# A written order for attention's instructions, value products in one block, and a rounded query that a transfer copies

## The chip, the cores and the metric

The kernel runs on one core of a Trainium2 chip. The metric is the device time of one execution in microseconds, the median of several runs; before the change it is 939.33 us (three runs, 938.42 to 941.68).

## What is computed

Three blocks follow each other on a batch of 4 sequences of 576 tokens. Attention with a decay has 8 heads of 64 per sequence, so 32 heads in all:

```
scores = scale * q @ k^T ; decay = cum[i] - cum[j], cum = cumsum(log(clip(f)))
attn   = exp(masked(scores + decay) - max) ; attn /= sum + 1e-9 ; out = attn @ v
```

Then comes a Fourier mixing over tokens and channels with a normalisation and a two-layer feed-forward (`u + relu(un @ w_ch1) @ w_ch2`), and last a block that multiplies by cos and sin of `x @ w_theta`, mixes over tokens with two 576 x 576 matrices, and gates. Every matmul in which 32-bit accuracy counts is split into high and low rounded parts.

## The kernel before, in words

`phase1` does attention and the Fourier transforms, `phase2` the feed-forward, `phase3` the last block. Attention goes head by head, heads in pairs (g = 0 and 1), four pairs to a sequence, 16 pairs in all.

For a head n, one transfer loads `raw` (keys and queries, transposed, twice over 128 partitions; `load_head`, L209, two buffers). `prep_units` rounds it to `hi` on ScalarE (L222), copies the rounded query's first 64 partitions to `q2` on ScalarE as well (L224; `q2` has one buffer for each g), and takes the remainders on GpSimd: the query's into the second half of `hi` (L226), the key's into `kl` (L228). `score_units` makes the score tiles of five row blocks, two matmuls each: `hi` by `hi` (L247), then `q2` by `kl` (L248), into PSUM banks named `pa` (three buffers). VectorE adds the mask and finds the row's extreme (L256, results `P` and `mn`), ScalarE takes the exponential (L261). `turn_units` transposes the 15 blocks of `P` on TensorE into banks `pb` (L286, three buffers), and four copies (three on VectorE, one on ScalarE, L289) bring them to `PT`. `av_units` then multiplies a pair's `PT` by its values `v` into `pt` (L321): 14 matmuls of 64 rows by 64 to 384 columns, the two heads on the two halves of the array's columns. `spread` turns the sums' reciprocals (`wide`, L267) into `R` (L300, L301), and `evac_pair` multiplies `pt` by `R` on VectorE (L347), moves single rows by small transfers (L356 to L363) and adds pairs up on GpSimd (L367, L370). After every fourth pair `fft_units` (L380 to L475) does that sequence's transform; GpSimd, ScalarE and VectorE prepare it, and its matmuls (L428, L439, L451) go between those of the next heads.

The order of the instructions on each engine is made by a scheduler in the tile framework, which simulates the program on a timeline and takes calls by priority. In `score_units` and `av_units` a priority is raised, and in `av_units` a pair's first value product is given a dependency on all eight `PT` copies of its two heads, so that the block does not begin before them. `p1_open`, with the first two heads, and most of `phase2` and `phase3` stand in the order in which they are written (`manual_schedule`). Transfers are issued by SyncE (SP), which issues in order and holds each until what it waits for is done; this includes waits for free buffers.

At the end, heads 30 and 31 overlap with the first normalisation (`norm_units`: `s` on GpSimd, L722, L735 on TensorE, a square root on ScalarE L742, a reciprocal on VectorE L745, L747 on TensorE, L754 to L756) and with the decoding of the first weights (L580 to L594). The feed-forward's first matmul is L767.

Of the kernel before, what the change touches and what calls it, by code (L numbers as in the profile page):

```python
# [17 lines left out]
B, H, S, D = 4, 8, 576, 64  # L18
# [35 lines left out]
G = 4  # L54


def f(ap):
    return ap.bitcast(F32)


class Net:
# [37 lines left out]
    def p1_open(self):  # L99
# [41 lines left out]
        for z in self.q2:  # L141
            nc.gpsimd.memset(f(z[64:66]), 1.0)
# [5 lines left out]
        for z in (self.xh, self.xl):  # L148
            nc.gpsimd.memset(f(z), 0.0)
# [123 lines left out]
    def turn_units(self, hd):  # L273
        nc = self.nc
        P = hd["P"]
        PT = self.w3.tile([128, 1600], F32, tag="PT", name="PT", bufs=4)
        hd["PT"], hd["copies"] = PT, []
        for bank, pieces in enumerate(TURNED):
            ps = self.bank_b()
            for j, a, b, off in pieces:  # L280
                for i in range(5):
                    if not a <= TOP[i] < b:
                        continue
                    o, n = off + TOP[i] - a, END[i] - TOP[i]
                    src = P[0:n, POFF[i] + KEY[j] : POFF[i] + KEY[j] + 128]
                    nc.tensor.transpose(ps[:, o : o + n], src, self.ident[0:n, 0:n])  # L286
            d, w = TSKIP[bank], TWIDE[bank]
            dst = PT[:, PTOFF[bank] : PTOFF[bank] + w]
            copy = nc.scalar.copy(dst, ps[:, d : d + w]) if bank > 2 else nc.vector.tensor_copy(dst, ps[:, d : d + w])  # L289
            hd["copies"].append(copy)  # L290
            yield

    def spread(self, p, T, wide):
# [10 lines left out]
    def av_units(self, m, hds, T, wide, done):  # L304
        nc = self.nc
        v = hds[0]["pair"]["v"]
        place = {
            (j, max(a, 128 * j)): PTOFF[bank] + off - TSKIP[bank] + max(a, 128 * j) - a
            for bank, pieces in enumerate(TURNED)
            for j, a, b, off in pieces  # L310
        }
        yield
        first = True
        with self.tc.high_priority(100):
            for j in range(5):
                for lo_q, hi_q in ((0, SPLIT), (SPLIT, 576)):
                    a = max(lo_q, 128 * j)
                    if a >= hi_q:
                        continue
                    for g in (1, 0):  # L320
                        ins = nc.tensor.matmul(  # L321
                            T[64 * g : 64 * g + 64, T0 + a : T0 + hi_q],
                            v[:, j, g, :],
                            hds[g]["PT"][:, place[j, a] : place[j, a] + hi_q - a],
                            start=j == 0,
                            stop=j == 4 or (j == 1 and hi_q == SPLIT),
                        )
                        if first:
                            for copy in hds[0]["copies"] + hds[1]["copies"]:
                                self.tc.add_manual_dep(  # L330
                                    ins.ins, copy.ins.name,
                                    mybir.DependencyInfo(mybir.DependencyClass.NoSync, mybir.DependencyReason.DATA),
                                    reason="one run",
                                )
# [143 lines left out]
    def phase1(self):  # L478
        pair, heads = self.p1_open()
        NH = B * H  # L480
        pairs, heads, raws = {0: pair}, dict(enumerate(heads)), {}
        fft = None
        self.tick = 0
        rows, norm, av = iter(()), iter(()), iter(())

        def pull():
            nonlocal fft
            next(rows, 0)
            self.tick += 1
            if self.tick % 3 == 0:  # L490
                next(norm, 0)
            if (self.tick % 5 or n > 24) and fft is not None and next(fft, 0) == 0:
                fft = None

        def done(m, T, R):
            nonlocal rows, fft
            for _ in rows:
                pass
            rows = self.evac_pair(m % NP, R, T, m == B * NP - 1)
            next(rows, 0)  # L500
            if m % NP == NP - 1:
                fft = self.fft_units(m // NP, *self.EO, rows)

        for n in range(-1, NH + 1):
            a = self.score_units(heads[n + 1], (n + 1) % 2) if 0 < n + 1 < NH else iter(())
            prep = iter(())
            if n + 2 < NH:
                p, g = divmod(n + 2, 2)
                if n == 0:
                    pairs[1] = self.load_pair(1)  # L510
                if n >= 0:
                    heads[n + 2] = dict(pair=pairs[p], g=n + 2)
                    prep = self.prep_units(n + 2, pairs[p], raws.pop(n + 2), heads[n + 2])
                if n > 0 and g == 1 and p + 1 < B * NP:
                    pairs[p + 1] = self.load_pair(p + 1)
            if n + 3 < NH:
                raws[n + 3] = self.load_head(n + 3)
            m, odd = divmod(n - 2, 2)
            if m >= 0 and not odd:
                T = self.bank_t()  # L520
                av = self.av_units(m, [heads[2 * m], heads[2 * m + 1]], T, pairs[m]["rz"], done)
            t = self.turn_units(heads[n]) if 0 <= n < NH else iter(())
            if n == NH - 1:
                self.p1a.close()
                self.p2_open()
# [573 lines left out]
        self.pu0.close()  # L1099


def body(tc, ins, out):
# [106 lines left out]
```

## Time and profile before

| what | value |
|---|---|
| median of three runs | 939.33 us (938.42 to 941.68) |
| the profiled execution's own time | 940.95 us |
| its span, first to last instruction | 939.2 us |
| TensorE busy in the span | 894.1 us (95%) |
| VectorE, ScalarE, GpSimd busy | 606.7, 417.8, 326.3 us |
| attention's last value product ends | 252.3 us after the span's start |
| mean granted TensorE clock | 0.985 |

The profile is of one execution. A busy time is the union of an engine's instructions; those of TensorE are pipelined, and their modelled ends overlap the next start, so that TensorE's idle time is what was surely lost, and short losses between two matmuls can hide inside the busy time. "Waits" say on which instruction of which engine an idle stretch ended. "issue" is a stretch with no wait that the profile shows.

### The profile page before, as it was taken

The page shows a single profiled execution, that of the slowest core. Times are in us where ns is not written, and L with a number is a line of the kernel's source. Part 1 is how long each engine was busy: PE and PEld are TensorE (multiplying, and loading weights), DVE is VectorE, ACT ScalarE, POOL GpSimd, SP SyncE. Part 2 cuts the span into 40 slices and gives each one's busy share as a digit, 9 for nine tenths or more (in the row PEclk, how much of TensorE's full clock was granted, in tenths as well). Part 3 has the DMA queues.
Part 4 walks back from the last instruction along what each step waited for, and adds up shares of the span by engine and source line. Part 5 has one row for each costly group of instructions (what it writes and reads, how often), then busy time and mean ns, then how long its engine had stood idle before and what let it go on. Part 6 is the DMA issues. An engine that isn't in the chain of part 4 may idle for free.

```text
span 939.2 us, 15860 instructions
## 1 busy us (share of the span) xinstructions
PE 894.1 (95%) x5960; PEld 841.5 (90%) x5960; DVE 606.7 (65%) x1495; ACT 417.8 (44%) x1014; POOL 326.3 (35%) x369
## 2 busy tenths in 40 slices
PE   4998999989788999999999999999999999999998
PEld 3777878777577999999999999999999999999998
DVE  8676676674899943456654565536687756747563
ACT  6888678685544332222221232223235534434331
POOL 6676788676601343000000000000035635425330
PEclk9999999999979999999999999999999999999999
DMA  5643423231233300013322122514310000010001
GB/s 167 202 149 106 130 93 114 83 105 40 82 97 93 90 1 1 1 46 90 91 91 90 45 90 74 199 29 127 109 51 2 1 26 27 14 40 1 26 27 51
DMA packets 23725, 68.04 MB, mean 72 GB/s; under 512 B 2906, under 2 KB 6362, under 8 KB 23648
## 3 DMA queue, kind: packets, MB, share of 16 engines
q1 hardware_dynamic: 20608, 62.88, 21.2%
q0 software_dynamic: 2320, 2.97, 1.2%
q10 hardware_dynamic: 720, 1.18, 0.4%
q8 instruction: 47, 0.77, 0.3%
q14 instruction: 30, 0.25, 0.1%
HBM read 57.91 MB, written 9.07 MB: 71 GB/s over the span
## 4 chain that ended last, share of the span: by engine, by line
PE 62%; DVE 5%; ACT 1%; issue 1%; DMA 0%; POOL 0%; DVEq 0%; SPq 0%; ACTq 0%
PE pa L767 19%; PE pb L781 11%; PE po L781 8%; PE pb L988 7%; PE pa L999 5%; PE pa L952 5%; PE po L988 5%; PE pa L948 1%; DVE u L789 1%; DVE kra L959 1%; DVE a L587 0%; DVE a L585 0%; DVE uc L754 0%; DVE kra L962 0%; PE pb L952 0%
## 5 line engine op out<-in xcount | busy, mean ns | idle before, releaser
L767 PE MATMUL pa<-un,wf 128*128 128x384 f32 x1152 | 221.4, 342 | 6.3 <-ACT un L755 3.4
L767 PEld LDWEIGHTS pa<-un,wf 128*128 128x128 f32 x1152 | 204.6, 191 | 10.2 <-DVE un L756 4.5
L773 DVE SCALAR_TENSOR_TENSOR h<-pa,h 128x384 fp32r<-128x384 f32 x96 | 52.4, 555 | 139.0 <-ACT h L772 139.0
L781 PE MATMUL pb<-h,wf 128*128 128x384 f32 x660 | 134.2, 337 | 0.3 <-DVE u L789 0.3
L781 PEld LDWEIGHTS pb<-h,wf 128*128 128x128 f32 x660 | 116.0, 188 | 1.1 <-DVE u L789 0.6
L781 PE MATMUL po<-h,wf 128*128 128x384 f32 x492 | 105.2, 340 | 0.4 <-ACT h L772 0.2
L772 ACT ACTIVATE h<-pa 128x384 fp32r<-128x384 f32 x96 | 45.7, 489 | 132.7 <-PE pa L767 130.0
L261 ACT ACTIVATE P<-P,mn 128x448 f32<-128x448 f32 (+4 forms) x160 | 89.0, 558 | 33.6 <-DVE mn L256 33.4
L988 PE MATMUL pb<-wtk,z 128*128 128x288 f32 x513 | 98.3, 295 | 1.3 <-ACT z L977 1.3
L944 POOL COPY xd<-u 128x64 f32<-128x64 f32 x32 | 6.9, 255 | 264.5 <-DVE u L789 254.5
L256 DVE CUSTOM_DVE_ANT_0 P<-pa,mask 128x448 f32<-128x448 f32 (+3 forms) x160 | 69.4, 457 | 42.1 <-PE pa L248 35.6
L781 PEld LDWEIGHTS po<-h,wf 128*128 128x128 f32 x492 | 86.2, 188 | 3.6 <-ACT h L772 1.9
L978 POOL TENSOR_TENSOR z<-kra,z 128x256 fp32r<-128x256 f32 x72 | 53.1, 752 | 93.5 <-ACT z L977 93.4
L247 PE MATMUL pa<-hi 128*128 128x448 f32 (+1 forms) x192 | 65.8, 364 | 20.5 <-DVE hi L226 9.4
L988 PEld LDWEIGHTS pb<-wtk,z 128*128 128x128 f32 x513 | 79.3, 188 | 2.0 <-ACT z L977 2.0
L988 PE MATMUL po<-wtk,z 128*128 128x288 f32 x351 | 75.2, 295 | 0.8 <-ACT z L977 0.8
L286 PE MATMUL pb<-ident,P 128*128 128x128 f32 (+2 forms) x480 | 73.9, 284 | 1.7 <-DVE uc L724 0.9
L247 PEld LDWEIGHTS pa<-hi 128*128 128x128 f32 x192 | 38.2, 204 | 30.1 <-issue 14.5
L289 DVE COPY PT<-pb 128x448 f32<-128x448 f32 (+1 forms) x96 | 55.6, 594 | 14.2 <-PE pb L286 13.3
L952 PE MATMUL pa<-wf,xs 128*128 128x256 f32 x456 | 64.1, 289 | 0.0
L286 PEld LDWEIGHTS pb<-ident,P 128*128 128x128 f32 (+2 forms) x480 | 56.6, 147 | 7.5 <-ACT P L261 1.2
L248 PE MATMUL pa<-kl,q 66*128 66x448 f32 (+1 forms) x192 | 58.0, 337 | 1.4 <-POOL kl L228 0.7
(206 smaller groups left out, 1667.0 us busy)
## 6 DMA issues: line engine op xcount, KB each, us to landing
raw<-in_qk SPq DMA_DIRECT2D x31, 576.0 KB
raw<-in_wf SPq DMA_DIRECT2D x32, 512.0 KB
raw<-in_wtk SPq DMA_DIRECT2D x18, 288.0 KB
v<-in_vp SPq DMA_DIRECT2D x16, 320.0 KB
out<-ob SPq DMA_DIRECT2D x12, 288.0 KB
dft<-in_dft POOLq DMA_DIRECT2D x8, 346.0 KB, 5.4
raw<-in_wth SPq DMA_DIRECT2D x4, 512.0 KB
st_wth<-raw SPq DMA_DIRECT2D x4, 512.0 KB
```

Source lines behind the costliest of these rows:

```text
L247: nc.tensor.matmul(t[:, 0 : b - a], hi[:, 1, q], hi[:, 0, a:b], start=True, stop=False)
L248: nc.tensor.matmul(t[:, 0 : b - a], q2[:, q], kl[:, g, a:b], start=False, stop=True)
L256: nc.vector.tensor_tensor_reduce(out=p[:, a:b], in0=t[:, 0 : b - a], in1=self.mask[:, m0 + a : m0 + b], scale=-0.125, scalar=least, op0=AL ...
L261: nc.scalar.activation(p, p, AF.Exp, bias=lowest, scale=-1.0, accum_out=zs[:, g, i : i + 1])
L286: nc.tensor.transpose(ps[:, o : o + n], src, self.ident[0:n, 0:n])
L289: copy = nc.scalar.copy(dst, ps[:, d : d + w]) if bank > 2 else nc.vector.tensor_copy(dst, ps[:, d : d + w])
L767: nc.tensor.matmul(ps[:, 0:CH], t[:, l, 128 * d : 128 * d + 128], un[r][:, d], start=n == 0, stop=n == 11)
L773: nc.vector.scalar_tensor_tensor(h[:, 1], ps[:, 0:CH], 0.0, f(h[:, 0]), ALU.max, ALU.subtract)
L781: nc.tensor.matmul(outs[d], t[:, l, 128 * d : 128 * d + 128], h[:, r], start=k % G == 0 and n == 0, stop=k % G == G - 1 and n == 2,)
L952: nc.tensor.matmul(th, xs[:, l, d], self.wth[d][:, r, 256 * hf : 256 * hf + 256], start=n == 0, stop=n == 11)
L978: nc.gpsimd.tensor_tensor(z[:, 1], t, f(z[:, 0]), ALU.subtract)
L988: nc.tensor.matmul(acc[k][th], z[:, l, 128 * k : 128 * k + 128], self.wtk[kt][:, r, 288 * th : 288 * th + 288], start=first and i == 0 and ...
```

## The change

Three things are changed.

First, all calls of attention from the first loop round up to the start of the round for head 31 are not given to the framework at once: a `Recorder` stands in the place of `nc`, keeps each call, and `emit` plays the calls in an order that a table of digits gives (each digit says which of the calls that are left comes next), under `manual_schedule`. So the scheduler no longer orders them. Calls before (the first two heads) and after (head 31's transposes, the last value products, the last transform, everything of `phase2`) are handled as before. Since the `Recorder`'s own line makes the recorded calls, they have line L71 in the changed kernel.

Second, the dependency of a pair's first value product on the eight copies is gone; in the table a pair's 14 value products follow each other.

Third, from head 2 on `q2` is filled by a transfer that SyncE issues, from `hi`, in the place of ScalarE's copy from `raw`.

```diff
@@ class Recorder (new)
+class Recorder:
+    def __init__(self, nc):
+        self.nc, self.calls, self.live = nc, [], True
+    def __getattr__(self, name):
+        return Queue(self, name)
+    def emit(self, order):
+        for k in order:
+            engine, name, a, kw = self.calls[k]
+            getattr(getattr(self.nc, engine), name)(*a, **kw)
+        self.live = False
+class Queue:
...
+    def __getattr__(self, name):
+        def call(*a, **kw):
+            if not self.rec.live:
+                return getattr(getattr(self.rec.nc, self.engine), name)(*a, **kw)
+            self.rec.calls.append((self.engine, name, a, kw))
+        return call
@@ prep_units
-        nc.scalar.copy(q2[0:64], raw[0:64, 1])
+        if n < 2:
+            nc.scalar.copy(q2[0:64], raw[0:64, 1])
+        else:
+            nc.sync.dma_start(f(q2[0:64]), f(hi[0:64, 1]))
@@ turn_units
-            copy = nc.scalar.copy(dst, ps[:, d : d + w]) if bank > 2 else nc.vector.tensor_copy(dst, ps[:, d : d + w])
-            hd["copies"].append(copy)
+            (nc.scalar.copy if bank > 2 else nc.vector.tensor_copy)(dst, ps[:, d : d + w])
@@ av_units
-                        if first:
-                            for copy in hds[0]["copies"] + hds[1]["copies"]:
-                                self.tc.add_manual_dep(
-                                    ins.ins, copy.ins.name,
...
-                            first = False
@@ phase1
         NH = B * H
+        rec = self.nc = Recorder(self.nc)
...
             if n == NH - 1:
+                with self.tc.manual_schedule():
+                    rec.emit(order(0, len(rec.calls)))
+                self.nc = rec.nc
                 self.p1a.close()
@@ the table and its reader (new)
+ORDERS = (
+    (
+        "&~$6~+X~,e~,e~,e~,e#*35=)129*6+1(%-((,yz%..#%+#$*&)$//()//%,:-#9C%/#]5/84<##U##,,6,$/4/3//$+44.)*881"
...
+def order(part, n):
+    left, taken, digits = list(range(n)), [], iter(ORDERS[part])
+    for c in digits:
+        k = DIGITS.find(c)
...
+        taken.append(left.pop(k))
+    return taken
```

Three places show what the table does. A row is one or more equal instructions, in the order in which their engine meets them; `pa` and `pb` are banks of scores and transposes, `pt` a pair's value products, `kl,q` the second score matmul, and P_107 and P_108 the `P` of even and odd heads.

On TensorE, around the value products of pair 5 (heads 10 and 11), before:

```order
L247 MATMUL pa<-hi 128x66
L248 MATMUL pa<-kl,q_99 128x66
L286 MATMUL pb<-ident,P_108 128x128 x3
L321 MATMUL pt<-PT,v 64x192 x2
L321 MATMUL pt<-PT,v 64x384 x2
L321 MATMUL pt<-PT,v 64x64 x2
L321 MATMUL pt<-PT,v 64x384 x2
L247 MATMUL pa<-hi 128x448
L247 MATMUL pa<-hi 128x128
L247 MATMUL pa<-hi 128x448
...
L321 MATMUL pt<-PT,v 64x320 x2
L321 MATMUL pt<-PT,v 64x192 x2
```

and of the change:

```order
L71 MATMUL pb<-ident,P_108 128x128
L71 MATMUL pb<-ident,wide 128x126
L71 MATMUL pa<-hi 128x448
L71 MATMUL pb<-ident,wide 128x128 x2
L71 MATMUL pt<-PT,v 64x192 x2
L71 MATMUL pt<-PT,v 64x384 x2
L71 MATMUL pt<-PT,v 64x64 x2
L71 MATMUL pt<-PT,v 64x384 x2
L71 MATMUL pt<-PT,v 64x320 x2
L71 MATMUL pt<-PT,v 64x192 x2
L71 MATMUL pt<-PT,v 64x64 x2
L71 MATMUL pb<-dft,oh 128x256 x2
```

The block stood right behind the odd head's last transposes, and six score matmuls cut it; now it is whole, and the scores (`pa`) and transposes (P_108) ahead of it belong to later heads, 13 and 14. Over the program the value products stand in 25 runs before and in 16 in the change.

On SyncE, transfers for heads 8 to 11 (`raw` of a head, `kl` rows and `v` of a pair, `q` the new copy), before:

```order
L209 DMA raw_508<-in_qk 128x1152
L203 DMA kl_592<-scr_94 2x2x576
L209 DMA raw_596<-in_qk 128x1152
L204 DMA v_426<-in_vp 128x640
L209 DMA raw_678<-in_qk 128x1152
L356 DMA x384_639<-Y_637 1x576
L357 DMA Y_637<-Y_637 1x16x36
L209 DMA raw_763<-in_qk 128x1152
```

and of the change:

```order
L71 DMA kl_291<-scr_94 2x2x576
L71 DMA raw_293<-in_qk 128x1152
L71 DMA v_254<-in_vp 128x640
L71 DMA q21_100<-hi_302 64x576
L71 DMA raw_312<-in_qk 128x1152
L71 DMA x384_305<-Y_304 1x576
L71 DMA q20_99<-hi_319 64x576
L71 DMA Y_304<-Y_304 1x16x36
```

One more transfer per head, 30 in all, stands among the loads, some of them behind the row moves of `evac_pair` or behind a `v` load.

On TensorE, at the end of attention (`P_108` here is head 31's), before:

```order
L286 MATMUL pb<-ident,P_108 128x128 x3
L300 MATMUL pb<-ident,wide 128x66
L300 MATMUL pb<-ident,wide 128x126
L300 MATMUL pb<-ident,wide 128x128 x2
L321 MATMUL pt<-PT,v 64x192 x2
...
L321 MATMUL pt<-PT,v 64x64 x2
L735 MATMUL pb<-mean,s_2995 128x1 x3
L747 MATMUL pb<-ident,rs 128x128 x3
L767 MATMUL pa<-un,wf 128x384 x14
```

and of the change:

```order
L329 MATMUL pb<-ident,wide 128x66
L329 MATMUL pb<-ident,wide 128x126
L329 MATMUL pb<-ident,wide 128x128 x2
L329 MATMUL pa<-ident,wide 128x128
L82 MATMUL pb<-mean,s_815 128x1 x3
L349 MATMUL pt<-PT,v 64x192 x2
...
L349 MATMUL pt<-PT,v 64x64 x2
L771 MATMUL pb<-ident,rs 128x128 x3
L791 MATMUL pa<-un,wf 128x384 x12
```

The normalisation's three column sums now stand ahead of the last pair's value products instead of behind them.

## Rows read from the trace of the kernel before

**Rows 1.** The page's head and its first part: busy us, share, instructions.

```profile
span 939.2 us, 15860 instructions
...
PE 894.1 (95%) x5960; PEld 841.5 (90%) x5960; DVE 606.7 (65%) x1495; ACT 417.8 (44%) x1014; POOL 326.3 (35%) x369
```

**Rows 2.** Stretches: length, busy us (count) of PE, PEld, DVE, ACT, POOL; clock, DMA, GB/s.

```profile
33.00:46.00 13.00, 12.22 (x99) 9.82 (x97) 9.52 (x36) 10.46 (x33) 10.63 (x11) 1.00 0.60 181
46.00:90.00 44.00, 41.55 (x337) 33.10 (x338) 33.69 (x126) 40.02 (x114) 29.94 (x25) 1.00 0.46 144
90.00:210.00 120.00, 110.79 (x870) 92.53 (x866) 80.87 (x285) 90.96 (x257) 90.92 (x86) 0.99 0.33 103
210.00:252.30 42.30, 38.63 (x285) 29.70 (x285) 25.83 (x81) 21.90 (x62) 30.16 (x30) 0.96 0.16 48
252.30:268.70 16.40, 9.67 (x34) 7.59 (x33) 15.07 (x29) 8.61 (x18) 2.77 (x4) 0.58 0.33 97
...
310.00:939.20 629.20, 623.11 (x4051) 617.11 (x4049) 375.24 (x798) 204.44 (x447) 137.98 (x171) 1.00 0.17 54
```

**Rows 3.** TensorE's waits, 33 to 252.3 us: total, times, longest.

```profile
PE pa L247 <- POOL hi L226: 3.5, 2, 2.6
PE pa L247 <- DVE mn L256: 3.2, 8, 0.8
PE pt L321 <- DVE PT L289: 3.2, 5, 1.3
PE pa L247 <- ACT R L301: 1.1, 2, 0.7
```

**Rows 4.** The weight load's waits, same stretch.

```profile
PEld pt L321 <- issue: 10.1, 50, 0.4
```

**Rows 5.** TensorE's timeline around pair 5's value products: start, us, what, [idle].

```profile
87.85 0.55 PE L286 MATMUL pb<-ident,P 128*128 128x128 f32 x3
89.74 1.95 PE L321 MATMUL pt<-PT,v 128*64 128x192 f32 x16 [1.34 <-DVE PT L289]
```

**Rows 6.** Groups of instructions, 33 to 252.3 us, ScalarE: busy, mean ns.

```profile
L222 ACT CAST hi<-raw 128x1152 fp32r<-128x1152 f32 x27 | 31.0, 1149 | 6.7 <-POOL Y L358 3.2 <-issue 2.2 <-POOL oo L397 0.7
...
L224 ACT CAST q<-raw 64x576 fp32r<-64x576 f32 x27 | 18.1, 670 | 0.0
```

**Rows 7.** The same view, GpSimd.

```profile
L228 POOL TENSOR_TENSOR kl<-raw,hi 64x576 fp32r<-64x576 f32 x28 | 39.6, 1413 | 2.1
L226 POOL TENSOR_TENSOR hi<-raw,hi 64x576 fp32r<-64x576 f32 x28 | 39.6, 1413 | 15.8 <-ACT hi L222 7.9 <-issue 4.5 <-POOL O L370 1.0
```

**Rows 8.** SyncE's timeline: small transfers issued and the next that waits for them.

```profile
55.28 0.26 SPq L356 DMA_DIRECT2D x<-Y  x1
56.47 0.58 SPq L357 DMA_DIRECT2D Y<-Y  x1
...
77.87 0.56 SPq L361 DMA_DIRECT2D x<-Y  x1
81.01 0.50 SPq L362 DMA_DIRECT2D Y<-Y  x1
```

**Rows 9.** The page's DMA queues: packets, MB, share of 16 engines.

```profile
q1 hardware_dynamic: 20608, 62.88, 21.2%
```

**Rows 10.** Busy time by stretch, two stretches at the lower clock.

```profile
145.80:149.20 3.40, 3.40 (x16) 3.31 (x16) 2.25 (x10) 3.07 (x14) 3.32 (x4) 0.51 0.00 0
210.60:214.00 3.40, 3.40 (x17) 1.67 (x18) 0.00 (x0) 1.39 (x6) 3.40 (x4) 0.50 0.34 95
```

**Rows 11.** TensorE's timeline at the end of attention.

```profile
249.42 2.93 PE L321 MATMUL pt<-PT,v 128*64 128x192 f32 x28 [0.36 <-DVE PT L289]
252.28 0.83 PE L735 MATMUL pb<-mean,s 128*128 128x1 f32 x6
255.74 1.65 PE L747 MATMUL pb<-ident,rs 128*128 128x128 f32 x6 [2.62 <-DVE rs L745]
259.94 0.69 PE L767 MATMUL pa<-un,wf 128*128 128x384 f32 x1 [2.55 <-ACT un L755]
```

More of the change, by code (lines that the diff above doesn't have):

```diff
@@ L58, in f, with __init__ @@
     return ap.bitcast(F32)
+class Recorder:
[9 more added lines that the diff above has]
+class Queue:
+    def __init__(self, rec, engine):
+        self.rec, self.engine = rec, engine
+    def __getattr__(self, name):
[4 more added lines that the diff above has]
+        return call
 class Net:
@@ L276, in turn_units @@
         PT = self.w3.tile([128, 1600], F32, tag="PT", name="PT", bufs=4)
-        hd["PT"], hd["copies"] = PT, []
+        hd["PT"] = PT
         for bank, pieces in enumerate(TURNED):
@@ L312, in av_units @@
         yield
-        first = True
         with self.tc.high_priority(100):
@@ L320, in av_units @@
                     for g in (1, 0):
-                        ins = nc.tensor.matmul(
+                        nc.tensor.matmul(
                             T[64 * g : 64 * g + 64, T0 + a : T0 + hi_q],
@@ L327, in av_units @@
                         )
-                        if first:
-                            for copy in hds[0]["copies"] + hds[1]["copies"]:
-                                self.tc.add_manual_dep(
-                                    ins.ins, copy.ins.name,
-                                    mybir.DependencyInfo(mybir.DependencyClass.NoSync, mybir.DependencyReason.DATA),
-                                    reason="one run",
-                                )
-                            first = False
         for _ in range(5):
@@ L1099, in phase3 @@
         self.pu0.close()
+DIGITS = "#$%&()*+,-./0123456789:;<=>?@ABCDEFGHIJKLMNOPQRSTUVWXYZ[]^_`abcdefghijklmnopqrstuvwxyz|"
+ORDERS = (
+    (
+        "&~$6~+X~,e~,e~,e~,e#*35=)129*6+1(%-((,yz%..#%+#$*&)$//()//%,:-#9C%/#]5/84<##U##,,6,$/4/3//$+44.)*881"
+        "*8815>6)=/T)2)))~*R~*R)/.33))$(#&D#/&+&#%%)&(((7?U&7=7CC%DD5:G555=5E6O6;%MNL94V4744:;58BFB5JA8777=$L"
+        "ECJDYP<O$G$$K?$$$$/$$>=$$$$$((:#&&((;#&&#51$09$8tu%0;%$$$22%%*%&($&&$%A=$%>;(((%&86;%:AA69:66>>5;&@&"
+        ":&$%1%%%$$7$5/$$($$$)$,###<5555)4)))$;#==/9(&&&+&(928))((&34&-66,#66%***;+%***#2/381*/$*0..DD)-DDI&H"
+        "(NN)*>+$***?G9F?CIWD(=Ua)@77$B6M<L6;%6$57OH4477%@%%$=$/$$$A?8$$$$$$$&6#%&3&&%%&3%2&&70%5%%.4&3,&&&&6"
+        ",;((+(%1H#).$-%BD(+B(%&*%$(%&&=6<%BB6:6:6??55;&@;&&$2%%%%$7$$/$$($+$$$##%#4$3#225%1%%%9.8&%%%*%44&81"
+        "7((&&%2%,66+%66*.**;%****33:+%0+(#/+--D-(BDD//(.+-)&:@$?(II9&8HH=88<)8L6))=)));)1$&&&->3&&*&&&),#((>"
+        "%=(<&;%.%-:7-??6#,--:--0.7>>,///-@@9%+,1==;%0-//+111/2.,54%2EEE:DD)23O-6P6-.,+2,11111EEE1DRR$*PB**M<"
+        "-O=N*MMMM*LL;9:*DD#V8UUUDTBS7RRBBBaQa#NAST%QR5fQQK>&&&2:&&&#%%%%%A%%%%$8B$<#;--9D44*6B4A?#4###(%&,&&"
+        "#AA)Q$P$#%%-%9%+8+#**3*@*AA$+)***N9$M~(?F*JN*I()$(3(&&&&.&[[(((&**&)5))$((0(T(%(,((&&?)>++&**$T??8DD"
+        "9$8889:7>>9;9@M;8K(J%I&6G&&&F&&&A.&&%%%%%%,&A+<5#:**+7+7+%*$*7((5FF)((2,((*/=***$:*9&)))4)3)(((H$:&&"
+        "(((&9#8(&6T6&5%%%%%0%%I%$,$%%%%$<<%((O(8(HH8$776II6B6$5O5CDD>5%4E66=664LLQ$34445F3E$$$B1P$$$$-K,;$$*"
+        "$7$$$$&#%%%D77%%%%%2&7%6&&#B%2$$*446%5)uu)~%3)+)8~%/.7%~%,.:)~%))$22(H&G,(+-+DD//(.$-*(OA%9?F(E9=99<"
+        "EE9?8*IA**&$((2((&&&2<1&&*&&&&,#%%&;;@#::.9...@6?&$?-,,,$/+,>5=//&.+8-&1);;$<<*+---1131+-715,%2;;;::"
+        "*283E-IGH-*-E+DD,CCCEEECDRR$*PB**M;>=UU*TTTT*SS;9:*DD#__8^DDIZBeQd7BbFaaaa$6_%UVOOYQN>&U&&2K$%%%%%%3"
+        "%%%%%=%$##9=68--64@@5*O@~(^3M?3###9#(((#&A*2**>*#@@L#K$&^+7++$***5#+L++<)*$K*-**GGJ(a$`E)))B)).W)WW)"
+        "=))&WW$^^P&^^))R`)R)%(&&L&&N&(M(K(&&,$K+(]**S%$Q77(66;KKX77966(R5((B((((>((-;(((((*H#)99))*6***+$7Q("
+        "(5))9(82,((*3***(:%)8)))5<*(:$(=888((((4(((*#&P)-))&(F&EP%%NaE%%%$$$$$$:$%%B%$$N474666JJ7%dM%%D1JD%%"
+        "%%$$$,+a$$$$$%4#X$$$0$$.$$$+&&&$R55%$33&2&&&:/9#P&%%%*%&817((&&%2%,#44*$44)))9__$~$[)7~$Y))~$W)9*0$~"
+        "$R/.*0..DD.)OD&CLV(U)?*+$***CPP;:9ISbL(al??)$86777?;7::=6BNRNWNBB%AAI;$EOMTFS%>%%1@%L%/%%A%0%%%B%%%."
+        "8.#-$,--;;-,,D8C$+(+4+++-:-Y-+--NOo+,,2,m,,++555+44&83*;;229#U312242<1;2::IZZ#JJ&IIGHHHHO^^jHi/8E#77"
+        "B7777QC77Y666#J555$##N**0~$;000~$1~$210~$@##D#~$?#%A%%#$&&~$6&$#$$$t#%#$$%%###~$.#j#####&&#%%%$$$$$)"
+        ")$((($&&&&$L((J((((F(((,$++K++I++++7J&C7GM&L5)**2)))KK$)))$()7((((8(2D)C#+3+++5<(;%#2QQ$(((&(&#0#**-"
+        "**/A/+..C$BHH<KKA.#--#<,,,,%#*&)#(((((1(3(%#-%%-$%+%%#%#%###"
+    ),
+)
@@ L1102, in body @@
+def order(part, n):
+    left, taken, digits = list(range(n)), [], iter(ORDERS[part])
+    for c in digits:
+        k = DIGITS.find(c)
+        if k < 0:
+            k = DIGITS.index(next(digits)) * len(DIGITS) + DIGITS.index(next(digits))
+        taken.append(left.pop(k))
+    return taken
 def body(tc, ins, out):
```

## The prediction

> **What bounds the kernel now.** I read the stretches first, then the waits of TensorE, then timelines at the places where a wait is long. The page's head gives the frame: TensorE is busy 894.1 of 939.2 us [rows 1]. By stretches, everything after 310 us is 99% full (623.1 of 629.2 us), and no edit touches it [rows 2]. What is open lies in attention. From 33 us on, when the first heads are through, to 252.3 us, when the last value product ends, TensorE is idle 0.78 + 2.45 + 9.21 + 3.67 = 16.1 us [rows 2]. From 252.3 to 268.7 us, where attention gives way to the feed-forward, it is idle 16.40 - 9.67 = 6.7 us [rows 2]. No other engine is full over all of attention. ScalarE comes nearest, 40.0 of 44 us (91%) from 46 to 90 us, before any transform has come in; there TensorE is busy 41.6 us, so the two run nearly level [rows 2].
>
> The idle 16.1 us is many small stops. The four largest kinds are a score matmul that waits for GpSimd's remainder (3.5 us in two waits, one of them 2.6 us), a score matmul whose bank VectorE has not yet read (3.2 us in eight), a value product that waits for `PT` copies (3.2 us in five), and a bank held by `R` (1.1 us) [rows 3]. So a new order can win some 10 us here and hardly more than 20. That is the scale of the whole question, 1 to 2%. (A measurement of this kernel tells a difference of about 0.3% or more, 2.8 us, from no change.)
>
> **The change part by part.** The arithmetic stays the same; on TensorE the change adds and removes no matmul. Each term is a stop that goes or comes.
>
> *Value products that wait for copies.* Before, the block stood right behind its odd head's last transposes; at pair 5 the transposes are through at 88.40 us, and the first product starts at 89.74, 1.34 us idle [rows 5]. The order of the change puts later heads' scores and transposes between, except for the last pair, whose place the scheduler still chooses. All such waits are 3.2 us [rows 3]; the last pair's 0.36 us [rows 11] stays. I take 2.8 us. Bounds: 0 if another wait takes the place, 3.2.
>
> *Whole blocks.* The order shows 25 runs of value products before and 16 now: nine cuts are gone. A cut costs an entry to the 64-column matmuls and a way back. No row prices it directly; the weight loads of these matmuls stood still without a visible cause 50 times for 10.1 us, 0.2 us each [rows 4]. At 0.2 us a cut the gain is 1.8 us. If all 10.1 us belonged to the 25 entries, it would be 0.4 us each and 3.6 us; the lower bound is 0. I take 1.8, since the 50 stops are more than the entries, and so some lie inside blocks.
>
> *The rounded query.* ScalarE loses a copy of 670 ns per head, 18.1 us in 27 of the 30 heads [rows 6]. Beside work elsewhere that is worth little: over 90 to 210 us ScalarE is busy 91.0 of 120 us [rows 2]. From 46 to 90 us TensorE's idle 2.45 us contains the 1.34 us counted above, so at most 1.1 us is left for it; I take 0.5 us, bounds 0 and 1.1. `raw` does not come free sooner by it, since GpSimd's two operations, 1.41 us each, read `raw` after the copy [rows 7].
>
> What it adds is 30 transfers of 64 x 576 x 4 bytes = 147 KB on SyncE's queue. The trace has no such transfer. Near ones: 2.3 KB row moves let the next transfer go 1.19 us (55.28 to 56.47) and 3.14 us (77.87 to 81.01) after their own issue [rows 8]. The queue moved 62.88 MB in 21.2% of 16 engines' 939.2 us [rows 9], 50.7 engine-us per MB; 0.147 MB on 16 engines is 0.47 us. So it takes between 1.7 and 3.6 us from issue, and I take 2.5, the middle, as the two rows lie equally near. The matmul that reads `q2` also reads `kl`, and GpSimd needs 2 x 1.41 = 2.83 us after the same rounding before `kl` is there [rows 7]. So up to 2.8 us the transfer is hidden behind GpSimd; I cost it at nothing. At 3.6 us it would show 0.8 us per head if nothing else covered it: the bound is a loss of 30 x 0.8 = 24 us. On SyncE, behind each such transfer stand the loads of `raw`, `kl` and `v` for heads one or two ahead. The place of a load in the new order allows for this; the cover is the head's time of lead, some 5.5 us a head in 46 to 90 us (8 heads in 44 us), and with it gone every load would add its lateness.
>
> The Trainium skill, page "DMA: Bandwidth & Descriptors", section "Anatomy of one DMA", gives a fixed 2.0 us and bytes / 436 GB/s for a transfer (fitted there on GpSimd's path), an estimate of 2.34 us here against ScalarE's 0.67 us, and so speaks against the edit: with nothing to hide it, 30 x 1.67 = 50 us would be lost. By the same figure it is hidden here, as the rows make it too.
>
> *Remainders.* With the copy off ScalarE and a new order on GpSimd, where remainders now stand between the sums of `evac_pair` and the transform more often than behind them, the two waits of 3.5 us [rows 3] should mostly go. I take 2.0 us, bounds 0 and 3.5.
>
> *Banks.* The waits on VectorE's reading and on `R`, 3.2 + 1.1 us [rows 3], I leave as they are. A score matmul must still find its bank read, three banks are there as before, and the new order puts no more matmuls between such a pair than the old one. Bounds: 3 us of gain, 3 us of loss.
>
> *Clock.* In two stretches of 3.4 us, from 145.8 and 210.6 us, the granted clock is 0.51 and 0.50, which is the 1.2 GHz level [rows 10]. Each costs 1.7 us of full-speed work. The second begins 0.4 us after the 2.6 us stop for GpSimd's remainder [rows 3]. If that stop goes, I expect the stretch to go with it: 1.7 us, bounds 0 and 3.4.
>
> *The end.* TensorE starts the column sums at 252.28 us, as the last block ends, and stands 2.62 us until the reciprocal is there at 255.74 [rows 11]. Now the sums stand ahead of the 2.93 us block, so 255.74 - 252.28 = 3.46 us of latency has 2.9 us of cover. I take 2.0 us. The rest of this handover (2.55 us for the first rounded part, and what follows) hangs on VectorE, busy 15.1 of 16.4 us [rows 2], and on row moves; I leave it. Bounds: 0, and all 6.7 us.
>
> The sum: 2.8 + 1.8 + 0.5 + 2.0 + 0 + 1.7 + 2.0 = 10.8 us. The profiled execution took 940.95 us in all, so it would take 930.2 us. It lies 1.6 us above the median of the three runs, 939.33, and so the median to expect is 928.5 us.
>
> **The rivals.**
>
> *More.* If the written order removes most of TensorE's stops rather than these few: 80% of the 16.1 us, with 3.6 us of cuts, 3.4 us of clock and 2 us at the end, 22 us, and 917 us. For it speaks that ScalarE, the fullest helper, gets 10% freer, and that the stops are spread over many kinds, which only a whole order can deal with. Against it speaks that three banks of each kind are still three.
>
> *Nothing.* The stops move. Where the table brings a block of 2.9 us whole, VectorE and ScalarE get no new scores in that time; and where the copies are no longer late, the banks are next. Eight bank waits cost 0.4 us each now [rows 3]; fifteen more would take 6 us, and if the remainders' waits and the clock stay too, 10.8 - 6.0 - 3.7 = 1.1 us is left: 938.2 us.
>
> *Slower: the query comes late.* SyncE issues in order; the copy for a head stands in places behind a row move that waits for `evac_pair`, or a `v` load that waits for a value product. If a transfer takes 3.6 us or stands behind such a wait, `q2` and not `kl` is what the score matmul waits for. It decides from the point where issue to landing exceeds 2.83 us. Its price is 24 us less the 10.8 us won, and the time 939.3 + 13.2 = 952.5 us. For it speaks the 3.14 us row; against it that the order leaves most of a head's scores and transposes between what SyncE waits for and the matmul that reads `q2`.
>
> *The table is without effect* cannot be: the order of each engine shows it.
>
> **How the numbers follow.** Forecast 0.50, more 0.20, nothing 0.18, late query 0.12. Faster by over 0.3%, below 936.5 us: 0.48 of the first, the 0.20, and 0.04 of the third, 0.72. Within 0.3%: 0.02 + 0.12 = 0.14. Slower: 0.02 of the third, which has losses too, and the 0.12, 0.14. The range takes in the forecast's bounds, the whole of the second case to a little beyond its 917 us, and the third to 940 us: 915 to 940 us, leaving out the late query and a little at the other end.
>
> **What would show it.** Right: from 33 us to the last value product TensorE idle near 8 us instead of 16.1; no wait of L71's value products for `PT` but the last pair's; the last value product some 8 to 9 us earlier than 252.3; the row for the query gone from ScalarE; a gap under 1 us between the last block and the reciprocal's matmuls; after 310 us the same work in the same 629 us. Wrong: score matmuls that wait for the DMA of `q`, more or longer bank waits, a new stretch at the lower clock, or a gain in attention that the handover at the end gives back because VectorE, with the decoding of weights, is late by as much.

## The result and the profile after

The changed kernel takes **931.33 us** (median of 4 runs, 930.24 to 932.45), the kernel before, beside it on the same chip, 940.5 us (938.42 to 941.81): 9.2 us less, a ratio of 0.9905 (0.988 to 0.993). The forecast was 928.5 us with a range of 915 to 940, that is 10.8 us less than a kernel before of 939.33. The profiled execution took 931.04 us, with a span 9.9 us shorter than the one before. The sum was right within 3 us, but it was so because its two parts, attention and the end, were wrong in opposite directions.

The page's head and its first part:

```profile
span 929.3 us, 15930 instructions
...
PE 890.6 (96%) x5960; PEld 842.2 (91%) x5960; DVE 610.2 (66%) x1495; ACT 402.9 (43%) x984; POOL 327.4 (35%) x369
```

ScalarE has 30 instructions less than before [rows 1], the queries' copies. The stretches, in the columns of [rows 2]:

```profile
31.00:46.00 15.00, 14.45 (x110) 11.43 (x108) 11.14 (x41) 12.20 (x38) 11.73 (x12) 1.00 0.64 190
46.00:90.00 44.00, 42.26 (x332) 34.10 (x330) 32.28 (x119) 34.50 (x102) 29.79 (x26) 0.96 0.60 178
90.00:200.00 110.00, 106.74 (x845) 89.36 (x847) 80.18 (x285) 81.46 (x239) 91.53 (x86) 1.00 0.43 131
200.00:239.10 39.10, 38.44 (x320) 32.03 (x316) 27.77 (x86) 24.87 (x67) 30.96 (x31) 1.00 0.21 68
239.10:255.40 16.30, 8.04 (x26) 6.33 (x27) 15.91 (x28) 7.87 (x16) 2.44 (x3) 0.71 0.22 68
...
300.00:929.30 629.30, 622.98 (x4055) 618.43 (x4053) 375.99 (x796) 204.65 (x446) 139.11 (x172) 1.00 0.16 53
```

From the first heads to the last value product TensorE is now idle 0.55 + 1.74 + 3.26 + 0.66 = 6.2 us, where it was 16.1 [rows 2]. The last 629.3 us are what they were. What TensorE still waits for, 31 to 239.1 us, and the weight load's stops (total, times, longest):

```profile
PE pa L71 <- DMA q<-hi: 2.5, 3, 1.7
PE pb L71 <- ACT PT L71: 1.2, 1, 1.2
...
PE pa L71 <- DVE mn L71: 0.2, 1, 0.2
```

```profile
PEld pt L71 <- issue: 11.4, 64, 0.2
```

The waits for remainders (3.5 us) and for `R` (1.1), and value products that wait for `PT` (3.2), are gone; the bank waits `pa <- DVE mn` fell from 3.2 to 0.2 [rows 3]. A new one came: score matmuls that wait for the query's transfer. Now TensorE's timeline from the last block on:

```profile
236.14 2.93 PE L349 MATMUL pt<-PT,v 128*64 128x192 f32 x28
239.00 0.93 PE L771 MATMUL pb<-ident,rs 128*128 128x128 f32 x6
243.24 0.69 PE L791 MATMUL pa<-un,wf 128*128 128x384 f32 x1 [3.30 <-ACT un L779]
...
249.76 0.62 PE L805 MATMUL po<-h,wf 128*128 128x384 f32 x2 [0.58 <-ACT h L796]
253.53 0.80 PE L448 MATMUL pb<-dft,eh 128*128 128x258 f32 x2 [3.15 <-ACT eh L421]
```

The block starts at 236.14 instead of 249.42 us [rows 11]: attention gained 13.3 us. Of these, 9.9 are stops (16.1 less 6.2), 1.7 are one stretch fewer at the lower clock level (below), and 1.7 remain for the cuts and for short losses inside the busy time. The span gained 9.9, so **3.4 us were given back behind it**. The same 60.6 us from the block on, before and after (columns as above), show it:

```profile
249.40:310.00 60.60, 50.78 (x284) 44.38 (x285) 57.81 (x118) 28.75 (x56) 9.15 (x10) 0.83 0.31 92
```

```profile
236.10:296.70 60.60, 47.56 (x264) 40.41 (x265) 55.63 (x112) 26.94 (x53) 7.44 (x7) 0.86 0.30 96
```

TensorE gets 20 matmuls less done in the same time, as it is busy 3.2 us less, at a clock no lower. The 2.62 us stop for the reciprocal [rows 11] is gone, as forecast, but a 3.15 us stop for `eh`, the rounded even half of the last transform, has come. (Counted over all stops, 1.5 of the 3.2 us are lost up to there, and the rest in smaller stops further on.) The chain to `eh` goes from the last pair's row moves on SyncE's queue to the sum `E` on VectorE and then to ScalarE's rounding. The moves, after, then before (start, us, what):

```profile
240.38 1.11 SPq L590 DMA_DIRECT2D raw<-in_wf  x2
241.61 0.53 SPq L381 DMA_DIRECT2D x<-Y  x1
246.09 0.50 SPq L382 DMA_DIRECT2D Y<-Y  x1
```

```profile
255.03 0.50 SPq L361 DMA_DIRECT2D x<-Y  x1
...
256.68 0.50 SPq L362 DMA_DIRECT2D Y<-Y  x1
```

The second move waits for the first. That is 1.65 us before and 4.48 us now, for the same 2.2 KB. Now two weight loads of 512 KB each were issued together, between 240.38 and 241.49 us, right ahead of it; before, the last load ahead of it had been issued by 253.07 us, some 2 us earlier, and alone.

But `eh` is not later than before, counted from the block. VectorE's sum `E`, and the matmul that reads `eh`, before:

```profile
262.54 0.74 DVE L367 TENSOR_TENSOR E<-X,Y 128x576 f32<-128x576 f32 x1
267.97 0.63 PE L428 MATMUL pb<-dft,eh 128*128 128x258 f32 x2
```

and VectorE ahead of `E` after the change (L606 and L607 decode the weights of the two loads):

```profile
245.02 0.42 DVE L606 TENSOR_SCALAR a<-a 128x512 f32<-128x512 f32 x1
...
246.58 0.73 DVE L606 TENSOR_SCALAR a<-a 128x512 f32<-128x512 f32 x1 [0.21 <-ACT a L604]
247.24 0.41 DVE L607 TENSOR_SCALAR a<-a 128x512 int32<-128x512 int32 x1
...
248.04 1.02 DVE L607 TENSOR_SCALAR a<-a 128x512 int32<-128x512 int32 x1
249.24 0.76 DVE L387 TENSOR_TENSOR E<-X,Y 128x576 f32<-128x576 f32 x1 [0.18 <-DMA Y<-x]
```

`E` starts 13.1 us behind the block's start in both kernels. TensorE, without the reciprocal's stop and with two feed-forward matmuls fewer in between, now comes to the matmul that reads `eh` 14.2 us behind the block's start, where it was 18.6, and finds it not yet there. And while the moves took longer, `E` itself stood only 0.18 us for the last of them: VectorE was busy 15.91 of the 16.30 us from 239.1 on.

### The profile page after: what moved, and what is told of

Its sections match the earlier page's. It is cut to its first block, busy times and chain, and to the rows that moved or that the text cites. A ratio compares the mean times of both kernels' runs of the same rounds, so it can differ in the third digit from the quotient of the medians.

```text
span 929.3 us, 15930 instructions
## 1 busy us (share of the span) xinstructions
PE 890.6 (96%) x5960; PEld 842.2 (91%) x5960; DVE 610.2 (66%) x1495; ACT 402.9 (43%) x984; POOL 327.4 (35%) x369
## 4 chain that ended last, share of the span: by engine, by line
PE 61%; DVE 6%; ACT 1%; issue 1%; POOL 0%; DVEq 0%; ACTq 0%
PE pa L791 20%; PE pb L805 12%; PE po L805 9%; PE pb L1012 6%; PE pa L1023 5%; PE pa L976 4%; PE po L1012 4%; DVE kra L983 1%; DVE kra L986 1%; PE pa L972 1%; DVE kra L985 1%; DVE kra L984 0%; DVE kra L982 0%; DVE kra L1000 0%; DVE u L813 0%
## 5 line engine op out<-in xcount | busy, mean ns | idle before, releaser
L71 ACT ACTIVATE P<-P,mn 128x576 f32<-128x576 f32 (+4 forms) x155 | 86.1, 557 | 34.1 <-DVE mn L71 33.5
L71 DVE CUSTOM_DVE_ANT_0 P<-pa,mask 128x448 f32<-128x448 f32 (+3 forms) x155 | 67.2, 459 | 29.9 <-PE pa L71 22.9
L71 PE MATMUL pb<-ident,P 128*128 128x128 f32 (+2 forms) x465 | 75.3, 284 | 2.5 <-ACT PT L71 1.2
L71 PE MATMUL pa<-hi 128*128 128x448 f32 (+1 forms) x186 | 63.2, 367 | 2.5 <-DVE mn L71 1.8
L71 PEld LDWEIGHTS pb<-ident,P 128*128 128x128 f32 (+2 forms) x465 | 56.0, 146 | 9.2 <-ACT PT L71 1.6
L71 DVE COPY PT<-pb 128x448 f32<-128x448 f32 (+1 forms) x93 | 53.4, 593 | 15.0 <-PE pb L71 12.3
L71 PE MATMUL pa<-kl,q 66*128 66x448 f32 (+1 forms) x186 | 55.5, 330 | 3.2 <-DMA q<-hi 2.5
L1012 PEld LDWEIGHTS po<-wtk,z 128*128 128x128 f32 x351 | 57.3, 188 | 1.2 <-ACT z L1001 1.2
```

The lines of the kernel that those rows point to most:

```text
L71: getattr(getattr(self.nc, engine), name)(*a, **kw)
L1012: nc.tensor.matmul(acc[k][th], z[:, l, 128 * k : 128 * k + 128], self.wtk[kt][:, r, 288 * th : 288 * th + 288], start=first and i == 0 and ...
```

## Experiments

Each run stood beside runs of the kernel before, whose median was 940.4 to 941.4 us each time; ratios are to those. The changed kernel's own ratio is 0.988 to 0.993, and a run whose interval overlaps that is not told from it by its time alone. Where a run's profile is read, it is one execution: in the four runs that share the changed kernel's attention (the changed kernel, 6, 7 and 8) the last block starts between 236.14 and 237.42 us.

**1 and 2. The transfer taken out, and the transfer alone.**

```diff
 q_on_scalare (the changed kernel, with)
-            nc.sync.dma_start(f(q2[0:64]), f(hi[0:64, 1]))
+            nc.scalar.copy(q2[0:64], raw[0:64, 1])
 before_q_dma (the kernel before, with)
-        nc.scalar.copy(q2[0:64], raw[0:64, 1])
+        (from head 2 on) nc.sync.dma_start(f(q2[0:64]), f(hi[0:64, 1]))
```

> The changed kernel with the written order kept, but the rounded query copied by ScalarE again, at the place that the transfer had in the order. Theory (the order makes the gain, the transfer is worth little): the three waits of score matmuls for the transfer, 2.5 us, go, and with the longest of them (1.7 us) the 3.4 us stretch at the lower clock that follows it, 1.7 us; ScalarE gets 30 x 0.67 us back and stands in the way of some exponentials, 2 to 4 us. Together 930 us, 928 to 934. Rival (ScalarE's relief is what the order lives on): more than half of the 9.2 us won is lost, 936 us or more.

> The kernel before, with the scheduler's order, and only the query's copy given to a transfer. Theory: within 2 us of the kernel before, 938 to 943 us, since TensorE waits for banks, remainders and copies of PT and hardly for ScalarE. Rival (relief of ScalarE): 4 us or more faster, 936 us or less. A third outcome, slower than 943 us, would say that the scheduler's queue of loads makes the transfer late.

Measured: 933.61 us (930.84 to 934.26), ratio 0.9919 (0.9901 to 0.9937), and 940.71 us, ratio 1.0002 (0.9987 to 1.0017). So the order makes nearly all of the gain, and the transfer in the old order none (in that run's profile the last block does start 2.5 us earlier than before, but the median of 12 runs shows nothing of it). In the first run the last block starts at 235.85 us, even 0.3 us before the changed kernel's; what its profile loses, it loses later: its span is 2.8 us longer, and behind 285 us it has two more stretches of 3.4 us at the lower clock level, each worth 1.7 us. Whether the copies cause those is open, and the 2.3 us between the two medians are not clear of noise. In attention, the 30 transfers as they stand are worth nothing net.

**3. The blocks cut again.** In each of 15 blocks the last 6 products are moved behind the next two TensorE calls that follow.

```diff
+ late = [o[i] for i in mine[8:]]
+ o[mine[8] : at] = [k for k in o[mine[8] : at] if k not in late] + late
```

> The changed kernel with 15 of its 16 blocks of value products cut in two, by the two matmuls that followed each: 31 runs where there were 16, all else in the same order. Theory (a cut costs 0.2 us): 15 x 0.2 = 3.0 us more, 934.3 us. If it is 0.4 us: 937.3 us. Rival (cuts cost nothing): 931.3 us.

Measured: 936.32 us (933.34 to 940.66), ratio 0.9959 (0.9943 to 0.9974). That is 5.0 us more than the changed kernel, 0.33 us a cut. In the profile the last block starts 5.3 us later (241.43 us), of which 1.2 us is a longer wait for the query (3.7 us in all, against 2.5), so about 0.27 us is the cut's own (the difference of the two medians is uncertain by some 3 us, 0.2 us a cut). The Trainium skill, page "TensorEngine Tiling (Array Packing)", section "Key Properties", says that changing the tiling mode drains the engine; the run fits that and puts a price on a cut, for which that section has no figure.

**4. The blocks whole, but earlier**, right behind their last `PT` copy.

```diff
+ at = 1 + max(position of the pair's PT copies, the last evac_pair, its v load)
+ o = rest[:at] + mine + rest[at:]
```

> The changed kernel with 15 of its blocks of value products moved up to right behind the last copy of PT that they read (or the reading of pt by the pair before, where that is later), still whole. Theory (waits for the copies were worth 2.8 us): most of it comes back, 0.2 us a block, about 3 us more, 934.3 us, with TensorE waits for VectorE's PT copies in the profile. Rival (the place of the block does not matter, since what is moved behind it fills in): 931.3 us within 1.5.

Measured: 947.23 us (945.84 to 951.13), ratio 1.008 (1.0059 to 1.0101): 15.9 us more than the changed kernel, slower than before. TensorE's waits in attention, 31 to 254 us:

```profile
PE pb L71 <- DVE PT L71: 5.6, 11, 1.0
PE pt L71 <- DVE X L71: 2.8, 5, 0.8
PE pb L71 <- ACT P L71: 1.9, 5, 0.6
...
PE pa L71 <- DVE mn L71: 1.4, 5, 0.5
PE pt L71 <- ACT PT L71: 0.7, 1, 0.7
```

The blocks themselves hardly wait for copies (0.7 us). It is the calls they used to part that wait now: transposes for a bank (5.6 us), value products for the bank of the pair before (2.8). A whole block is 2.9 us of work for TensorE that needs nothing recent. That its place decides which chain of the other engines it covers is the reading that fits these waits; that the place is worth more than the wholeness, the times show (15.9 us against 5.0).

**5. The table alone taken out**, the scheduler orders the recorded calls.

```diff
-                with self.tc.manual_schedule():
-                    rec.emit(order(0, len(rec.calls)))
+                rec.emit(range(len(rec.calls)))
```

> The changed kernel with the table alone undone: the same calls are recorded and then emitted in the program's order, and the scheduler orders them as before; the transfer stays, and so does the removal of the edit that held a value product for all copies. Theory (the table's order makes the gain): 939 to 943 us, no different from before, with TensorE's waits in attention at 15 us or more. Rival (what held the value products before was the added wait for all ten copies, and removing it makes the gain): 932 to 936.

Measured: 955.49 us (951.4 to 962.27), ratio 1.0159 (1.0128 to 1.019). Both expectations miss. (A pair's added wait was for eight copies; the ten in the text is a slip.) Without the table the change would be a loss of 14 us. TensorE's waits, 31 to 262 us:

```profile
PE pa L71 <- POOL hi L71: 7.7, 4, 4.0
PE pa L71 <- DVE mn L71: 7.5, 16, 0.7
```

The kinds are those of before, twice as long. Against before, this run has the transfer (nothing, run 2), no added wait, and all calls given to the scheduler at one moment; which of the last two costs the 14 us, no run tells.

**6 and 7. The late row moves on another queue.**

```diff
+            q = nc.gpsimd if last else nc.sync      # rows_on_scalare: nc.scalar
-            nc.sync.dma_start(self.x256, Y[64:65])
+            q.dma_start(self.x256, Y[64:65])
 (and the two moves behind it alike)
```

> Theory: after the change the last pair's first row move lands 4.5 us after its issue (241.61 to 246.09 us) because two weight loads of 512 KB were issued just ahead of it on SyncE's queue at 240.38; before, the same move took 1.65 us. On GpSimd's queue nothing stands ahead of it: the sum E starts near 246.5 instead of 249.24, TensorE's 3.15 us wait for the rounded even half at 253.53 shrinks to under 1, and the time is about 928.5 us (927.5 to 930). Rival: the queue is not what delays it (the engines that carry the bytes are shared, or VectorE reaches E late anyway): the move still takes over 4 us or the wait stays, and the time is 931 to 932.

> Same theory, the three row moves issued by ScalarE: the first should land in under 2 us, but ScalarE stands at each issue until the row before has landed, with the casts of the next stage behind it. Theory: 929 to 931 us, a little worse than on GpSimd's queue. Rival (the queue does not matter): 931 to 933.

Measured: 931.7 us (929.87 to 933.95), ratio 0.9903 (0.9887 to 0.9918), and 934.71 us (932.16 to 936.39), ratio 0.9926 (0.9909 to 0.9943). Neither is told from the changed kernel, and the queue is not what makes the move late. On GpSimd's and on ScalarE's, first and second move:

```profile
242.28 0.59 POOL L382 DMA_DIRECT2D x<-Y  x1 [1.61 <-DVE Y L367]
246.61 0.50 POOL L383 DMA_DIRECT2D Y<-Y  x1 [3.73 <-DMA x<-Y]
```

```profile
242.87 0.61 ACTq L382 DMA_DIRECT2D x<-Y  x1
247.74 0.50 ACTq L383 DMA_DIRECT2D Y<-Y  x1
```

The moves take 4.3 and 4.9 us there, too. The loads were under way on the same 16 DMA engines. In run 6 `E` starts 14.3 us behind the block with no wait for a row at all, VectorE being busy up to it, and TensorE's stop is for decoded weights (2.79 us at 253.51) instead of `eh`.

**8. The row moves ahead of the two loads.** The third and fourth weight load are held until the last row move is issued.

```diff
+            self.row = nc.sync.dma_start(Y[0:1], self.x384)
-        while self.nraw < 2 and self.raws:
+        while self.nraw < 2 and self.raws and not (self.begun == 2 and self.row is None):
+        if self.begun in (3, 4):
+            add_manual_dep(this load, self.row)
```

> The two runs with another queue have shown that the first row move takes 4.3 to 4.9 us on any queue while two 512 KB loads are under way. Here the last pair's three row moves stand ahead of the third and fourth weight load, so no load is under way. Theory (the loads' bytes delay the row moves, and those delay the even half that TensorE waits for): the first move lands in under 2 us, the sum E starts before 246 us after a block that starts near 236, the 3.15 us wait for the even half shrinks to under 1, and the time is 928 to 929.5 us. Rival (VectorE is the bound between 239 and 300 us, so what it does first does not matter): row moves and E are early, but TensorE then waits as long for the weights decoded later, and the time stays at 930.5 to 932.5.

Measured: 928.73 us (927.36 to 930.09), ratio 0.9866 (0.985 to 0.9883), 2.6 us less than the changed kernel. SyncE's timeline, and the 60.6 us from the last block on:

```profile
242.08 0.53 SPq L381 DMA_DIRECT2D x<-Y  x1
244.13 0.51 SPq L382 DMA_DIRECT2D Y<-Y  x1
246.00 0.24 SPq L383 DMA_DIRECT2D Y<-x  x1
246.35 13.33 SPq L591 DMA_DIRECT2D raw<-in_wf  x4
```

```profile
236.60:297.20 60.60, 51.62 (x283) 45.09 (x283) 55.83 (x112) 24.73 (x51) 7.63 (x7) 0.86 0.27 88
```

The second move follows after 2.05 us, no stop for `eh` is left, and TensorE gets 283 matmuls done, as before the change (284). The sum E starts 10.9 us behind the block's start, instead of 13.1, not the 10 expected, since VectorE is busy until then:

```profile
247.53 0.74 DVE L387 TENSOR_TENSOR E<-X,Y 128x576 f32<-128x576 f32 x1
...
250.66 0.43 DVE L613 TENSOR_SCALAR a<-a 128x512 f32<-128x512 f32 x1 [0.38 <-ACT a L611]
```

So these two loads cost most of the give-back by the medians (2.6 of 3.4 us), and less by the two profiles (1.5). This run's interval just touches the changed kernel's; run 11, where the same edit wins 4.5 us on top of run 10, is clear of noise. By which way they cost is not shown, since the edit moves two things at once. The row moves come early, and the decoding of the two loads on VectorE (L613 here), of which 2.6 us stood ahead of `E` in the changed kernel, now stands behind it. The 0.18 us for which `E` stood for its row there speaks for the decoding; in run 10, where attention ends earlier still, it stood 1.15 us, so that there the rows count too.

**9. The query's transfer ahead of loads.** The transfer that TensorE waits 1.68 us for at 56.11 us was issued at 49.98, behind loads (timeline of SyncE, then of GpSimd and of TensorE, of the changed kernel):

```profile
47.11 0.33 SPq L71 DMA_DIRECT2D raw<-in_qk  x1
49.56 0.33 SPq L71 DMA_DIRECT2D v<-in_vp  x1
49.98 0.47 SPq L71 DMA_DIRECT2D q<-hi  x1
```

```profile
47.03 1.45 POOL L71 DMA_DIRECT2D dft<-in_dft  x2
```

```profile
56.11 0.44 PE L71 MATMUL pa<-kl,q 66*128 66x448 f32 x1 [1.68 <-DMA q<-hi]
```

```diff
 for every head, in the table's order:
+ loads = [a v load since the last query, a raw load since this head's rounding]
+ o[i : j + 1] = [k for k in o[i : j + 1] if k not in loads] + loads
```

> Theory: the query transfer is late only where a value tile (320 KB) or a head's input (576 KB) was issued just ahead of it on SyncE's queue: the one issued at 49.98 us holds TensorE until 56.11. With the query's transfer ahead of those loads in the queue, TensorE's three waits for it (2.5 us) go, and with the longest of them the half-clock stretch at 58.09 that follows it (1.7 us lost): attention ends 2.5 to 4 us earlier, about 928 us (926.5 to 929.5). Rival: the query lands late for another reason (two buffers that are free late, the rounding itself): the waits stay and the time is 931 to 932; or the value tiles come late in their place: over 932.

> Both edits together (query transfers ahead of loads, the last pair's row moves on GpSimd's queue). If both theories hold and the gains add: about 925.5 us (924 to 928). If only one holds: 928 to 929. If neither: 931 to 932.

Measured: 930.06 us (928.81 to 935.4), ratio 0.9893 (0.987 to 0.9915); with run 6's edit 930.2 us (929.29 to 931.44), ratio 0.9884 (0.987 to 0.9899). Neither is told from the changed kernel. Of the waits 1.9 us stay: the one of 1.68 us shrinks to 0.42, and the one for the query before it grows from 0.32 to 1.44. The edit mainly moves the lateness. (The last block does start 2.2 us earlier in the first run's profile, at 233.92 us, where no stretch at the lower clock is left in attention; the times, 928.81 to 935.4, do not settle what that is worth.) The theory counted SyncE's loads alone. GpSimd had issued two loads of the transform's table, 346 KB each, at 47.03 us, and the edit leaves loads like these where they are; how much of the lateness is theirs, no run tells.

**10. The late queries by ScalarE, the others by transfer.**

```diff
-        if n < 2:
+        if n < 2 or n in (5, 7, 23):
             nc.scalar.copy(q2[0:64], raw[0:64, 1])
```

> The three queries that TensorE waits for (heads 5, 7 and 23) are copied by ScalarE, the other 27 by transfer. Theory: the three waits (2.5 us in all) and the half-clock stretch behind the longest (1.7 us) go for three copies on ScalarE, and the time is 927 to 929.5 us. Rival (ScalarE's copies delay its exponentials or bank copies at these places, as in the run with all copies on ScalarE, whose attention ended 0.3 us earlier but no more): 931 to 934.

Measured: **928.05 us** (927.59 to 928.31), ratio 0.9858 (0.9844 to 0.9873), 3.3 us less than the changed kernel. The wait left, 31 to 239 us:

```profile
PE pa L71 <- DMA q<-hi: 0.3, 1, 0.3
```

The last block starts at 232.53 us, 3.6 us earlier than with all by transfer and 3.3 earlier than with all by ScalarE (run 1). So by these profiles 27 transfers are worth 3.3 us in attention, stops and clock together, and three late ones take as much away.

**11. Both edits that helped.**

```diff
 q_mixed_rows = the edits of rows_before_loads and q_mixed
```

> The two edits that each gained 2.6 to 3.3 us over the changed kernel, together: heads 5, 7 and 23 copied by ScalarE, and the last pair's row moves ahead of the third and fourth weight load. They act in different stretches (before 165 us, and after 236 us). Theory (the gains add): 925 to 926.5 us. Rival (the handover is bound by VectorE once attention ends earlier still, or the half-clock stretches behind the handover fall worse): 927.5 to 929.

Measured: **923.54 us** (923.1 to 925.51), ratio 0.9819 (0.9806 to 0.9833). It beats both kernels, by 16.9 us and 7.8 us. The gains add, with some 2 us over, whose cause is open.

## Why the prediction was right, point by point

The sum was 8.8 us won in attention and 2.0 at its end. It was 13.3 won, and 3.4 lost.

*Value products that wait for copies* (2.8 us forecast): all 3.2 us are gone, with the last pair's. Right.

*Whole blocks* (1.8): the price of a cut was 0.2 us, from the weight load's stops [rows 4]. Measured 0.33, or about 0.27 net: 2.4 to 3.0 us for nine cuts. The change's own profile leaves 1.7 us for them and for all other short losses, so that 1.8 may have been the better size. That a cut costs is right, but the row was the wrong one: after the change, with no cut left, the stops are 64 and 11.4 us. They lie inside the blocks.

*The rounded query* (0.5 for ScalarE, 0 for the transfer): the working asked whether issue to landing exceeds 2.83 us, and bounded it with 1.7 to 3.6 us from two row moves, taken as equally near [rows 8]. They were not. The one of 3.14 us at 77.87 was issued 0.4 us behind a load of 576 KB, and so was the nearer to a query among loads:

```profile
77.45 0.33 SPq L209 DMA_DIRECT2D raw<-in_qk  x1
```

With 0.9 MB of loads just ahead on SyncE's queue, and the table's loads on GpSimd's, it was 6.1 us (49.98 to 56.11). The rival was right in what is then waited for, `q2` and not `kl`, and in its point of decision. What it gave as the cause, a wait of SyncE, was not the main one: the query's rounding ended at 49.31 us, and its transfer was issued 0.7 us later. And it came true for 3 heads of 30, so that its price was some 3.3 us (run 10), not 24.

*Remainders* (2.0): all 3.5 us went. Right, at the upper bound.

***Banks* (0)** is, within attention, the term that was mis-sized most: 3.2 + 1.1 us of waits fell to 0.2. The step that failed was to take the waits as unchanged because "the new order puts no more matmuls between such a pair than the old one". Counted in the two traces, that sentence is true: from the last matmul into a score bank to the first into the same bank again there are 22.3 matmuls on average before and 21.6 now, and 16 in the median of both. The waits fell all the same, so it is not their number that counts but what stands where. Run 4 shows how much the blocks' places alone do: moved, with all else in its order, they cost 15.9 us, of which 9.8 us are waits on banks and `X`. Which places made the waits of before go, no run tells.

*Clock* (1.7): the two stretches at the lower level in attention [rows 10] are gone, and one came: the 46 to 90 us row shows 0.96. It begins at 58.09 us, behind the 1.68 us stop for the query. One fewer of two, as forecast, by another road. In run 10, without that stop, none is left; but run 1, without it too, has one at 36.5 us (0.51), and the first of run 9, with a stop of 1.44 us, has none. So that the stop brings the stretch is not shown.

*The end* (2.0 won) has the wrong sign, 3.4 lost. The working was right that the reciprocal's stop goes. What failed is the step behind it: it named VectorE and the row moves, and then "I leave it". The next thing TensorE needs from that chain, `eh`, came no earlier, as `E` starts 13.1 us behind the block in both kernels, so that the 2.62 us won ahead of it were lost again in the 3.15 us stop, and more in the stops behind. The last lines of the prediction named just that, a gain that the end gives back because VectorE, with the decoding of weights, is late. Runs 8 and 11 show that the third and fourth load are behind a large part of it. Their edit moves the loads' bytes and their decoding together, so that it doesn't show which of the two holds `E`; the trace of the changed kernel, with VectorE busy 15.91 of 16.30 us, speaks for the prediction's reading.

That the two errors, 4.5 us too little in attention and 5.4 us too much at the end, nearly cancel is chance.

## What to carry to other kernels

When an order is written by hand, don't only keep its longest independent piece of work whole, but try its place, first where the other engines' chain is longest: here a worse place cost three times as much as a cut. A small transfer's cost is read from what the 16 DMA engines are carrying when it is issued, and not from its size or its queue; look at each place where it stands behind a large load, and keep the copy on an engine for those alone. And when a stop goes, follow the next stage's longest chain from the same starting point in both traces: if its end is no earlier, the next stop takes the gain. List what shares that chain's engines, here the loads and their decoding, and move it behind.

## What was not expected of the hardware

A move of 2.2 KB between partitions took 1.65 us in the kernel before, with the DMA engines 34% busy, 2.05 us in run 8, with them 1% busy, and 4.3 to 4.9 us behind 1 MB of loads, on SyncE's, GpSimd's and ScalarE's queue alike. While it waited, the DMA engines were 83% busy, and it was through when they fell idle (changed kernel, stretches):

```profile
241.00:243.00 2.00, 0.00 (x0) 0.00 (x0) 2.00 (x4) 0.89 (x2) 0.00 (x0) 0.85 0.83 195
243.00:245.00 2.00, 0.69 (x1) 0.29 (x1) 2.00 (x5) 1.02 (x3) 0.00 (x0) 0.50 0.83 331
245.00:247.00 2.00, 1.85 (x6) 1.85 (x7) 1.79 (x5) 1.78 (x5) 0.90 (x1) 0.50 0.01 4
```

The Trainium skill, page "DMA: Bandwidth & Descriptors", section "Queues, rings and completion order", says that each DMA engine takes turns between the queues it has work for, a packet at a time, where a packet is a group of typically 9 to 17 descriptors. Here an engine's share of one 512 KB load is, by an even split of the trace's 4 KB pieces, 8 of them, and so fits into one packet. By that rule a row on another queue can still have to wait for the load that is being moved, and runs 6 and 7 neither confirm nor contradict it. In the same page of the Trainium skill, the section "Issuing engines are not separate DMA queues" says that all transfers end on the same 16 engines, whichever engine starts them; runs 6 and 7 agree, with 4.3 and 4.9 us.
